# A retention layer feeding a two-matrix MLP: first loads spread over three queues, state sums ahead of outputs, and transposes and loads grouped by two pairs

## The chip, the cores and the metric

The kernel runs on one core of one Trainium2 chip. The metric is the device time of one execution in microseconds (us). Eight executions of the kernel before the change took 209.01 to 209.62 us, with a median of 209.3 us. One further execution was recorded by the profiler; it took 209.35 us, and its span, from the first to the last instruction, is 207.5 us.

## The reference

For each of 4 batch entries and 8 heads, a state of 64 x 64 is carried along 768 time steps. At each step it decays, takes up the outer product of k and v, and is read by q. The result, 3072 tokens of 512 features, goes through two matrices with x cos x between them.

```python
batch, n_heads, seq, head_dim = (4, 8, 768, 64)
n_tokens, d_model, d_ff = (3072, 512, 2048)

gamma = 1.0 - 2.0 ** (-5.0 - np.arange(H, dtype=np.float32))
scale = 1.0 / np.sqrt(D)
for t in range(S):
    state = gamma[None, :, None, None] * state + np.einsum('bhd,bhe->bhde', k[:, :, t], v[:, :, t])
    y[:, :, t] = scale * np.einsum('bhd,bhde->bhe', q[:, :, t], state)

h = x @ w_in          # x is y, heads side by side
g = h * np.cos(h)
out = g @ w_out
```

## The kernel before

The 768 steps are cut into six chunks of 128. Two batch entries are worked on together, so that there are 12 *pairs* p: two batch entries (b is 0 or 1) of one chunk, all eight heads. Pairs 0 to 5 are the six chunks of the first two entries, 6 to 11 those of the others. Decay is put into q and k beforehand, as powers of gamma, so that inside a chunk the recurrence becomes masked matrix products.

A pair goes through these steps, each a helper in the code:

- `load` brings q, k and v from memory, 256 KB for one b of one tensor. `load_k` brings both b of k in one transfer. A pair lands in one of five buffer slots, by the table `SLOT`.
- `conv_q`, `conv_k` and `conv_v` scale and turn to bf16: q and k into `qk`, v into `vs` (three buffers each, by p % 3). From pair 3 on q and v are converted on GpSimd (POOL) and k on ScalarE (ACT).
- `stage_t` transposes q and k of one b on TensorE (PE) and copies the result out on VectorE (DVE) into `qkt`. `stage_t_dma` does the same with two transposing transfers on SyncE's queue (SP). Pairs 0 to 3 use the first, 4 to 11 the second.
- `stage_a` is A, the products of k and q inside the chunk (two PSUM banks per b); `stage_m` multiplies them by the triangular mask on VectorE into `am`. `attend` is both, for both b.
- `half_y` is Y: the older state (`stb`) times q plus v times `am`, for one b; ScalarE copies the result into `xt`. `stage_s` is S: it adds the chunk's k-v products to the state in `st_ps` and copies it to `stb`. `stage_y` is Y of both b, then S.

Two pairs make a group g of 512 tokens for the MLP. `unit_f` computes one block f of 128 of the 2,048 hidden features for all 512 tokens; `act` takes the cosine on ScalarE and multiplies on VectorE into `gt`. `pair_f(p, r)` does four blocks for one pair alone (256 tokens), two blocks to a bank, and `first_f` for the first four blocks. `unit_o` multiplies `gt` with a quarter of `w_out` for 128 tokens; after the fourth quarter ScalarE copies the bank to `ob` and SP stores it. `warm` issues matrix products whose result nobody uses.

The program writes out the order of work on every engine by hand; each engine takes its instructions in that order, and an instruction whose input or buffer is not ready holds up those behind it. There are seven PSUM banks beside `st_ps`. `Banks.take` picks the bank that the written plan (`Clock`) expects to come free first; the numbers of `Clock` choose banks, not the order. The semaphores are put in from the data that instructions touch.

Around the change: in the beginning SP loads q and k of pair 0 and POOL the rest. S of pair 0 stands between the two Y of pair 0 on TensorE, and its copies behind the first `xt` copy on ScalarE. In the middle, q of pairs 4 and 5 and one v are loaded on SP, the rest on POOL; from pair 6 on POOL issues six loads for one pair, two conversions of q and two of v, then the next pair's six loads. The functions `ahead`, `fetch` and `later` place them at steps s of the main loop over groups.

Of the kernel before, what the change touches and what calls it, by code (L numbers as in the profile page):

```python
# [10 lines left out]
FP32 = mybir.dt.float32  # L11
# [36 lines left out]
def kernel(  # L48
# [32 lines left out]
    def sb(shape, dt, name):  # L81
        return const.tile(shape, dt, name=name)
# [14 lines left out]
    w_out_sb = sb([128, KOUT, DM], BF16, "w_out_sb")  # L97


    qf = [[sb([128, H, D], FP32, f"qf{i}_{b}") for b in range(2)] for i in range(PRE)]  # L100
    kf2 = [sb([128, 2, H, D], FP32, f"kf{i}") for i in range(PRE)]
    kf = [[t[:, b] for b in range(2)] for t in kf2]
    vf = [[sb([128, H, D], FP32, f"vf{i}_{b}") for b in range(2)] for i in range(PRE)]
    ob = [sb([128, DM], FP32, f"ob{i}") for i in range(4)]
    NB = 3
    qk = [sb([128, 2, 2, H, D], BF16, f"qk{i}") for i in range(NB)]
# [11 lines left out]
    gq = sb([128, NC, H], FP32, "gq")  # L118
    gk = sb([128, NC, H], FP32, "gk")
    rel = sb([128, 128], FP32, "rel")  # L120


    SRC = {"q": (qf, q), "k": (kf, k), "v": (vf, v)}
# [3 lines left out]
    def load(eng, p, names):  # L127
        bp, c = divmod(p, NC)
        for n in names:
            t, src = SRC[n[0]]  # L130
            b = int(n[1])
            eng.dma_start(  # L132
                out=t[SLOT[p]][b],
                in_=src[2 * bp + b, :, ds(c * C, C)].rearrange("h t d -> t h d"))

    def load_k(p):
        bp, c = divmod(p, NC)
        nc.gpsimd.dma_start(
            out=kf2[SLOT[p]].rearrange("p b h d -> p (b h) d"),
            in_=k[2 * bp : 2 * bp + 2, :, ds(c * C, C)].rearrange("b h t d -> t (b h) d"))  # L140

    def load_w_in(r):
        nc.gpsimd.dma_start(
# [14 lines left out]
    def w_in_t(i, f):  # L158
# [1 line left out]
        return w.rearrange("p (m j) -> p j m", j=4)[:, f % 4, :]  # L160


    load(nc.sync, 0, ("q0", "k0", "q1"))
    nc.gpsimd.iota(pos, pattern=[[C, NC]], base=1, channel_multiplier=1,
                   allow_small_or_imprecise_dtypes=True)
    nc.gpsimd.iota(rel, pattern=[[1, 128]], base=0, channel_multiplier=-1,
                   allow_small_or_imprecise_dtypes=True)
    load(nc.gpsimd, 0, ("k1",))
    load(nc.gpsimd, 1, ("q0", "q1"))
    load_k(1)  # L170
    load(nc.gpsimd, 0, ("v0", "v1"))
    nc.vector.memset(zero, 0.0)
    nc.vector.memset(lnsc, math.log(scale))
# [76 lines left out]
    def stage_a(p, b):  # L250
        n = p % NB
        bk = [banks.take(), banks.take()]
        ap = [t.rearrange("p (a t) -> p a t", a=HP) for t in bk]
        for a in range(HP):
            for j in range(2):
                po = 64 * j
                nc.tensor.matmul(ap[j][:, a, :], lhsT=kt(n, b, a)[po : po + 64, :],  # L257
                                 rhs=qt(n, b, a)[po : po + 64, :],
                                 tile_position=(po, 0))
        clk.run("pe", 0.3)  # L260
        return b, bk, ap, clk.pe

    def stage_m(p, item, parts=(0, 1)):
        b, bk, ap, done = item
        for j in parts:
            nc.vector.tensor_tensor(  # L266
                out=am[p % 2][b][j], in0=ap[j],
                in1=mask.unsqueeze(1).to_broadcast([128, HP, 128]), op=ALU.mult)
            banks.give(bk[j], clk.run("dve", 0.64, done + 0.1))

    def half_y(p, b):
        c = p % NC
        n = p % NB
        bank = banks.take()
        yp = bank.rearrange("p (a t) -> p a t", a=HP)
        for a in range(HP):
            if c > 0:
                for j in range(2):
                    nc.tensor.matmul(  # L279
                        yp[ts(j, 64), a, :], lhsT=stb[p % 2][:, b, a, ts(j, 64)],  # L280
                        rhs=qt(n, b, a), start=True, stop=False,
                        skip_group_check=True)
            for j in range(2):
                nc.tensor.matmul(  # L284
                    yp[ts(j, 64), a, :], lhsT=vs[n][:, b, 2 * a + j, :],
                    rhs=am[p % 2][b][j][:, a, :], start=(c == 0), stop=True,
                    skip_group_check=True)
        nc.scalar.copy(out=xt[(p // 2) % 2][:, :, ts(2 * (p % 2) + b, C)], in_=yp)  # L288
        clk.run("pe", 0.5)
        banks.give(bank, clk.run("act", 0.6, clk.pe + 0.1))  # L290

    def stage_s(p, copy_st):
        c = p % NC
        n = p % NB
        if c == NC - 1:
            return
        for b in range(2):
            for a in range(HP):
                for j in range(2):
                    h = 2 * a + j  # L300
                    nc.tensor.matmul(  # L301
                        st_ps[ts(j, 64), b, a, :], lhsT=qk[n][:, b, 1, h, :],
                        rhs=vs[n][:, b, h, :], start=(c == 0 and b == 0 and a == 0),
                        stop=True, skip_group_check=True)
        clk.run("pe", 0.25)
        if copy_st is not None:
            state_out(p, copy_st)
# [103 lines left out]
    def warm(n):  # L411
        for _ in range(n):
            nc.tensor.matmul(spare, lhsT=zero[:, :128], rhs=zero, start=True, stop=True,
                             skip_group_check=True)
        clk.run("pe", 0.3 * n)
# [47 lines left out]
    warm(1)  # L463
    clk.run("pe", 0.0, 11.8)
    stage_m(1, stage_a(1, 0))
    half_y(0, 0)
    clk.run("pe", 0.0, 12.4)
    stage_m(1, stage_a(1, 1))
    stage_s(0, nc.scalar.copy)
    half_y(0, 1)  # L470
    warm(3)
    half_y(1, 0)
    banks.give(spare, clk.pe)
    half_y(1, 1)
    stage_s(1, nc.scalar.copy)
# [6 lines left out]
    for u in range(12):  # L482
        unit_o(0, u % 4, u // 4)
        if u == 7:
            stage_t(2, 0)
            stage_t(2, 1)
            conv_v(2, nc.vector, (0,))
        elif u == 9:
            stage_m(2, stage_a(2, 0))
            conv_v(2, nc.vector, (1,))  # L490
        elif u == 11:
            stage_m(2, stage_a(2, 1))
    conv_k(3, True)
    conv_q(3, nc.gpsimd)
    load(nc.sync, 4, ("q0", "q1"))
    load(nc.gpsimd, 4, ("k0", "k1", "v0", "v1"))
    conv_v(3, nc.gpsimd)
    load(nc.sync, 5, ("q0", "q1", "v0"))
    load(nc.gpsimd, 5, ("k0", "k1", "v1"))
    for j in range(4):  # L500
        unit_o(0, j, 3)
        if j == 1:
            stage_y(2, nc.scalar.copy)
    pair_f(2, 0)
    stage_t(3, 0)
    stage_t(3, 1)
    pair_f(2, 1)
    attend(3)
    conv_q(4, nc.gpsimd)
    conv_v(4, nc.gpsimd)  # L510
    conv_k(4, True)
    stage_t_dma(4)
    load(nc.gpsimd, 6, ("q0", "k0", "q1", "k1", "v0", "v1"))
    pair_f(2, 2)
    pair_f(2, 3, (0,))
    stage_y(3, nc.scalar.copy)
    pair_f(2, 3, (1,))
    conv_q(5, nc.gpsimd)
    conv_v(5, nc.gpsimd)
    load(nc.gpsimd, 7, ("q0", "k0", "q1", "k1", "v0", "v1"))  # L520
    pair_f(3, 0)
    conv_k(5, True)
    stage_t_dma(5)
    pair_f(3, 1)
    pair_f(3, 2)
    conv_q(6, nc.gpsimd)
    conv_k(6, True)
    conv_v(6, nc.gpsimd)
    pair_f(3, 3)

    def ahead(p):
        if p < NP:
            conv_q(p, nc.gpsimd)
            conv_k(p, True)
            conv_v(p, nc.gpsimd)

    def fetch(p):
        load(nc.gpsimd, p, ("q0", "k0", "q1", "k1", "v0", "v1"))

    def later(p):  # L540
        stage_y(p)
        n = 8 if p == 4 else p + 3 if p > 5 else NP
        if n < NP:
            fetch(n)

    late = []

    def put_off(when, step):
        late.append((when, step))
# [13 lines left out]

    o_units(1, 0, 2)
    attend(4)
    stage_t_dma(6)
    o_units(1, 2, 6)
    later(4)
    attend(5)
    o_units(1, 6, 10)  # L570
    later(5)

    for g in range(2, NG + 1):
        for s in range(16):
            hf, r = divmod(s, 8)
            p = 2 * (g + 1) + hf
            if g == 2 and s % 2 == 0 and s < 12:
                unit_o(1, *divmod(10 + s // 2, 4))
            if g < NG:
                unit_f(g, s)  # L580
            if g > 2:
                if g < NG or s < 12:
                    unit_o(g - 1, *divmod(s, 4))
                elif s == 12:
                    last_o(g - 1, 3)
            while late and late[0][0] <= 16 * g + s:
                late.pop(0)[1]()
            if p < NP:
                if r == 0:
                    ahead(p + 1)  # L590
                elif r == 1:
                    if p + 1 < NP:
                        stage_t_dma(p + 1)
                elif r == 2 and p in (6, 7, 8):
                    todo = [stage_a(p, b) for b in range(2)]
                    stage_m(p, todo[0])
                    put_off(16 * g + s + 1, lambda todo=todo, p=p: stage_m(p, todo[1]))
                elif r == 6 and p in (6, 7, 11):
                    later(p)
                elif (g, s) == (3, 4):  # L600
                    fetch(11)
                if (g, s) in joined:
                    join(joined[g, s], 16 * g + s)


# [28 lines left out]
```

## Time and profile before

| what | value |
|---|---|
| median of 8 runs | 209.3 us (209.01 to 209.62) |
| profiled execution | 209.35 us, its span 207.5 us |
| TensorE busy | 201.2 us, 97% of the span |
| VectorE, ScalarE, GpSimd busy | 112.7, 114.3, 102.5 us |
| chain that ended last | 92% TensorE, 3% DMA, 2% VectorE |
| software queue (POOL's transfers) | 20.98 MB, 38.1% of 16 engines' span |
| hardware queue (SP's transfers, the transposes among them) | 12.49 MB, 26.2% |
| clock granted to TensorE | 1.00 |

Busy time of an engine is the union of its instructions; for TensorE their ends are modelled. The chain of waits goes back from the last instruction, at each step to what released it or to the instruction before it on its engine. A timeline row gives the start and length of some instructions in a row, what they write and read, and in brackets how long the engine was idle before and what ended that. The landing time of a transfer is from its issue to its last byte; the answers give the least, the median and the largest of those asked for.

### The profile page before, as it was taken

To read this page: it belongs to the slowest core of one execution; us is meant where nothing else is said; L and a number is where in the kernel's file an instruction comes from. 1 tells how busy PE (TensorE), PEld (TensorE's weight loads), DVE (VectorE), ACT (ScalarE), POOL (GpSimd) and SP (SyncE) were. 2 spreads that over 40 slices of the span, in tenths; PEclk is the share of its full clock that TensorE was granted. 3 is DMA by queue.
4 is the path that set the end of the run, shared out by engine and by line. 5 is a ranking of instruction groups with operands and counts; after the bars stand their busy time and mean duration, and the time that the engine had idled before them with its cause. 6 is when DMAs were issued, how large, how long until landed. Compare 5 with 4: busy or idle time off the path is not lost.

```text
span 207.5 us, 4176 instructions
## 1 busy us (share of the span) xinstructions
PE 201.2 (97%) x1646; PEld 113.3 (55%) x1646; DVE 112.7 (54%) x188; ACT 114.3 (55%) x193; POOL 102.5 (49%) x118
## 2 busy tenths in 40 slices
PE   7889999999999999999999999999999999999993
PEld 3357554558997555546544466444465444444452
DVE  4691984544957454869874466853467244443000
ACT  6677872257996336577653754653554653553120
POOL 8999238399999999999998030000000000000000
PEclk9999999999999999999999999999999999999999
DMA  6999999999999999979997411161101100110212
GB/s 153 336 241 202 215 241 287 335 279 328 252 218 280 293 216 298 215 244 181 210 272 243 121 37 48 57 101 51 51 3 51 51 20 34 51 52 21 80 75 79
DMA packets 36644, 33.83 MB, mean 163 GB/s; under 512 B 26768, under 2 KB 29072, under 8 KB 36624
## 3 DMA queue, kind: packets, MB, share of 16 engines
q0 software_dynamic: 7808, 20.98, 38.1%
q1 hardware_dynamic: 28672, 12.49, 26.2%
q8 instruction: 13, 0.21, 0.4%
q10 hardware_dynamic: 144, 0.10, 0.1%
q14 instruction: 7, 0.06, 0.1%
HBM read 27.26 MB, written 6.29 MB: 162 GB/s over the span
## 4 chain that ended last, share of the span: by engine, by line
PE 92%; DMA 3%; DVE 2%; issue 1%; SPq 0%; ACT 0%; DVEq 0%
PE bank L379 39%; PE bank L338 32%; PE bank L349 7%; PE bank L257 3%; DMA qf<-in_q_dram 3%; PE bank L279 3%; PE bank L284 3%; PE bank L396 2%; PE st_ps L301 1%; DVE am L266 1%; PE bank L360 1%; PE bank L230 1%; PE bank L367 1%; DVE qkt L214 1%; SPq L132 0%
## 5 line engine op out<-in xcount | busy, mean ns | idle before, releaser
L331 DVE TENSOR_TENSOR gt<-bank,cosb 128x512 bf16<-128x512 f32 x96 | 64.8, 688 | 62.3 <-ACT cosb L327 62.0
L327 ACT ACTIVATE cosb<-bank,halfpi 128x512 bf16<-128x512 f32 x96 | 65.1, 688 | 49.9 <-PE bank L338 45.5
L379 PE MATMUL bank<-w_out_sb,gt 128*128 128x512 bf16 x368 | 89.6, 379 | 0.0
L338 PE MATMUL bank<-xt,w_in 128*128 128x512 bf16 x304 | 75.3, 380 | 0.0
L379 PEld LDWEIGHTS <-gt 128*128 128x128 bf16 x368 | 35.4, 98 | 41.3
L338 PEld LDWEIGHTS <-w_in 128*128 128x128 bf16 x304 | 33.7, 114 | 30.9
L266 DVE TENSOR_TENSOR am<-bank,mask 128x512 bf16<-128x512 f32 x48 | 30.4, 682 | 4.2 <-PE bank L257 4.2
L202 POOL TENSOR_TENSOR vs<-vf,gk 128x512 bf16<-128x512 f32 x21 | 21.4, 1041 | 7.3 <-PE st_ps L301 7.2
L386 ACT COPY ob<-bank 128x512 f32<-128x512 f32 x23 | 13.4, 586 | 18.1 <-PE bank L379 18.0
L132 POOL DMA_DIRECT2D vf<-in_v_dram x23 | 20.2, 884 | 4.5 <-DMA w_out_sb<-in_moe_w_out_dram 4.5
L195 POOL TENSOR_TENSOR qk<-qf,gq 128x512 bf16<-128x512 f32 x18 | 18.8, 1068 | 2.9 <-DMA qf<-in_q_dram 2.2
L132 POOL DMA_DIRECT2D kf<-in_k_dram x21 | 18.9, 900 | 1.8 <-DMA w_out_sb<-in_moe_w_out_dram 1.6
L208 ACT CAST qk<-kf 128x512 bf16<-128x512 f32 x24 | 13.9, 615 | 9.2 <-DMA kf<-in_k_dram 9.2
L288 ACT CAST xt<-bank 128x512 bf16<-128x512 f32 x24 | 13.0, 588 | 7.7 <-PE bank L284 7.6
L132 POOL DMA_DIRECT2D qf<-in_q_dram x18 | 16.2, 901 | 1.3 <-DMA w_in<-in_moe_w_in_dram 1.3
L349 PE MATMUL bank<-xt,w_in 128*128 128x256 bf16 x128 | 14.7, 273 | 0.0
L349 PEld LDWEIGHTS <-w_in 128*128 128x128 bf16 x128 | 13.8, 114 | 0.4
L284 PE MATMUL bank<-am,vs 128*64 128x128 bf16 x192 | 11.7, 220 | 0.0
L279 PEld LDWEIGHTS <-stb 128*64 128x64 bf16 x160 | 8.8, 109 | 4.3 <-issue 3.1
L279 PE MATMUL bank<-qkt,stb 128*64 128x128 bf16 x160 | 10.7, 222 | 0.1
L284 PEld LDWEIGHTS <-vs 128*64 128x64 bf16 x192 | 10.0, 110 | 0.5 <-issue 0.4
L313 DVE CAST stb<-st_ps 64x512 bf16<-64x512 f32 x12 | 8.2, 684 | 2.7 <-PE st_ps L301 2.6
(46 smaller groups left out, 87.0 us busy)
## 6 DMA issues: line engine op xcount, KB each, us to landing
vf<-in_v_dram POOLq DMA_DIRECT2D x23, 256.0 KB, 6.2
out_dram<-ob SPq DMA_DIRECT2D x23, 256.0 KB, 2.0
kf<-in_k_dram POOLq DMA_DIRECT2D x21, 256.0 KB, 6.5
qf<-in_q_dram POOLq DMA_DIRECT2D x18, 256.0 KB, 5.9
w_out_sb<-in_moe_w_out_dram POOLq DMA_DIRECT2D x4, 512.0 KB, 12.4
qf<-in_q_dram SPq DMA_DIRECT2D x6, 256.0 KB, 7.7
w_in<-in_moe_w_in_dram POOLq DMA_DIRECT2D x3, 512.0 KB, 8.7
kf<-in_k_dram POOLq DMA_DIRECT2D x1, 512.0 KB, 5.9
```

The source lines that it names most:

```text
L132: eng.dma_start(out=t[SLOT[p]][b], in_=src[2 * bp + b, :, ds(c * C, C)].rearrange("h t d -> t h d"))
L195: eng.tensor_tensor(out=qk[p % NB][:, b, 0], in0=qf[SLOT[p]][b], in1=bc(gq, p % NC), op=ALU.mult)
L202: eng.tensor_tensor(out=vs[p % NB][:, b], in0=vf[SLOT[p]][b], in1=bc(gk, p % NC), op=ALU.mult)
L208: nc.scalar.copy(out=qk[p % NB][:, b, 1], in_=kf[SLOT[p]][b])
L266: nc.vector.tensor_tensor(out=am[p % 2][b][j], in0=ap[j], in1=mask.unsqueeze(1).to_broadcast([128, HP, 128]), op=ALU.mult)
L279: nc.tensor.matmul(yp[ts(j, 64), a, :], lhsT=stb[p % 2][:, b, a, ts(j, 64)], rhs=qt(n, b, a), start=True, stop=False, skip_group_check=True)
L284: nc.tensor.matmul(yp[ts(j, 64), a, :], lhsT=vs[n][:, b, 2 * a + j, :], rhs=am[p % 2][b][j][:, a, :], start=(c == 0), stop=True, skip_grou ...
L327: nc.scalar.activation(out=cb, in_=bank, func=AF.Sin, bias=halfpi)
L331: nc.vector.tensor_tensor(out=out, in0=bank, in1=cb, op=ALU.mult)
L338: nc.tensor.matmul(bank, lhsT=w_in_t(i, f), rhs=xt[g % 2][:, i, :], start=(i == 0), stop=(i == KIN - 1))
L349: nc.tensor.matmul(bank[:, ts(e, 256)], lhsT=w_in_t(i, f + e), rhs=xt[g % 2][:, i, ts(hf, 256)], start=(i == 0 and e == 0), stop=(i == KIN ...
L379: nc.tensor.matmul(bank, lhsT=gt[g % 2][:, f, ts(j, 128)], rhs=w_out_sb[:, f, :], start=(f == 0), stop=(f == KOUT - 1))
```

## The change

- At the start, k of pair 0 (b = 0) is issued on ScalarE's hardware queue, ahead of ScalarE's first table load. SP issues q of pair 0 and then q of pair 1 (b = 0 each). The second q of pair 0 goes to POOL, behind the second k.
- S of pair 0 moves ahead of both Y of pair 0, and both Y behind both A of pair 1. Of the three `warm` products one stays ahead of pair 1's first Y and two go between its two Y.
- q, k and v of all slots become tiles that hold both b, and from pair 4 on each is loaded by one transfer of 512 KB on POOL (`load_both`). SP no longer loads in the middle.
- Pair 3 is transposed by transfers. A new function `turn` takes one or two pairs: q conversions, transposing transfers of all of them on SP, v conversions, then on POOL a copy of two elements (`gate`) out of the last pair's first transposed half, and behind that the loads for the next two pairs in the order k, q, k, q, v, v.
- The k conversions on ScalarE get places of their own: that of pair 3 at u = 9, that of pair 4 behind `pair_f(2, 0)`, that of pair 5 behind `attend(3)`, later ones by a table `k_at`. The tables `t_at`, `a_at` and `y_at` take the place of `ahead`, `fetch` and `later`.

```diff
-    load(nc.sync, 0, ("q0", "k0", "q1"))
+    load(nc.scalar, 0, ("k0",))
+    load(nc.sync, 0, ("q0",))
+    load(nc.sync, 1, ("q0",))
...
-    load(nc.gpsimd, 0, ("k1",))
-    load(nc.gpsimd, 1, ("q0", "q1"))
-    load_k(1)
+    load(nc.gpsimd, 0, ("k1", "q1"))
+    load(nc.gpsimd, 1, ("q1",))
+    load_both(("k", 1))
...
     stage_m(1, stage_a(1, 0))
+    stage_s(0, nc.scalar.copy)
+    clk.run("pe", 0.0, 13.0)
+    stage_m(1, stage_a(1, 1))
     half_y(0, 0)
-    clk.run("pe", 0.0, 12.4)
-    stage_m(1, stage_a(1, 1))
-    stage_s(0, nc.scalar.copy)
     half_y(0, 1)
-    warm(3)
+    warm(1)
     half_y(1, 0)
+    warm(2)
     banks.give(spare, clk.pe)
     half_y(1, 1)
...
             conv_v(2, nc.vector, (1,))
+            conv_k(3, True)
...
-    conv_k(3, True)
-    conv_q(3, nc.gpsimd)
-    load(nc.sync, 4, ("q0", "q1"))
-    load(nc.gpsimd, 4, ("k0", "k1", "v0", "v1"))
-    conv_v(3, nc.gpsimd)
-    load(nc.sync, 5, ("q0", "q1", "v0"))
-    load(nc.gpsimd, 5, ("k0", "k1", "v1"))
+    def turn(ps, loads=()):
+        for p in ps:
+            conv_q(p, nc.gpsimd)
+        for p in sorted(ps):
+            stage_t_dma(p)
+        for p in sorted(ps):
+            conv_v(p, nc.gpsimd)
+        if loads:
+            nc.gpsimd.tensor_copy(out=gate, in_=qkt[max(ps) % NB][:, 0, 1, HP - 1, 126:])
+            load_both(*[(n, p) for n, p in (
+                ("k", 0), ("q", 0), ("k", 1), ("q", 1), ("v", 0), ("v", 1)) for p in [loads[p]]])
+
+    turn((3,), (4, 5))
...
     pair_f(2, 0)
-    stage_t(3, 0)
-    stage_t(3, 1)
+    conv_k(4, True)
     pair_f(2, 1)
     attend(3)
-    conv_q(4, nc.gpsimd)
-    conv_v(4, nc.gpsimd)
-    conv_k(4, True)
-    stage_t_dma(4)
-    load(nc.gpsimd, 6, ("q0", "k0", "q1", "k1", "v0", "v1"))
+    conv_k(5, True)
+    turn((5, 4), (6, 7))
...
+    k_at = {(2, 6): 8, (2, 9): 9, (3, 2): 10, (3, 12): 11}
+    t_at = {(2, 9): ((8, 9), (10, 11)), (3, 3): ((10,),), (3, 13): ((11,),)}
+    a_at = {(2, 2): 6, (2, 10): 7, (3, 2): 8}
+    y_at = {(2, 6): 6, (2, 14): 7, (4, 14): 11}
```

More of the change, by code (lines that the diff above doesn't have):

```diff
@@ L97 @@
     w_out_sb = sb([128, KOUT, DM], BF16, "w_out_sb")
[L100 to L103, printed above, removed]
+    both = {n: [sb([128, 2, H, D], FP32, f"{n}f{i}") for i in range(PRE)] for n in "qkv"}
+    qf, kf, vf = [[[t[:, b] for b in range(2)] for t in both[n]] for n in "qkv"]
     ob = [sb([128, DM], FP32, f"ob{i}") for i in range(4)]
@@ L120 @@
     rel = sb([128, 128], FP32, "rel")
+    gate = sb([128, 2], BF16, "gate")
     SRC = {"q": (qf, q), "k": (kf, k), "v": (vf, v)}
@@ L134, in load, with load_both @@
                 in_=src[2 * bp + b, :, ds(c * C, C)].rearrange("h t d -> t h d"))
[L136 to L140, printed above, removed]
+    def load_both(*names):
+        for n, p in names:
+            bp, c = divmod(p, NC)
+            nc.gpsimd.dma_start(
+                out=both[n][SLOT[p]].rearrange("p b h d -> p (b h) d"),
+                in_=SRC[n][1][2 * bp : 2 * bp + 2, :, ds(c * C, C)].rearrange(
+                    "b h t d -> t (b h) d"))
     def load_w_in(r):
@@ L517 @@
     pair_f(2, 3, (1,))
-    conv_q(5, nc.gpsimd)
-    conv_v(5, nc.gpsimd)
-    load(nc.gpsimd, 7, ("q0", "k0", "q1", "k1", "v0", "v1"))
     pair_f(3, 0)
-    conv_k(5, True)
-    stage_t_dma(5)
     pair_f(3, 1)
     pair_f(3, 2)
-    conv_q(6, nc.gpsimd)
-    conv_k(6, True)
-    conv_v(6, nc.gpsimd)
     pair_f(3, 3)
[L531 to L544, printed above, removed]
     late = []
@@ L565 @@
     attend(4)
-    stage_t_dma(6)
     o_units(1, 2, 6)
-    later(4)
+    conv_k(6, True)
+    stage_y(4)
     attend(5)
+    conv_k(7, True)
+    turn((6, 7), (8, 9))
     o_units(1, 6, 10)
-    later(5)
+    stage_y(5)
+    k_at = {(2, 6): 8, (2, 9): 9, (3, 2): 10, (3, 12): 11}
+    t_at = {(2, 9): ((8, 9), (10, 11)), (3, 3): ((10,),), (3, 13): ((11,),)}
+    a_at = {(2, 2): 6, (2, 10): 7, (3, 2): 8}
+    y_at = {(2, 6): 6, (2, 14): 7, (4, 14): 11}
     for g in range(2, NG + 1):
         for s in range(16):
-            hf, r = divmod(s, 8)
-            p = 2 * (g + 1) + hf
             if g == 2 and s % 2 == 0 and s < 12:
@@ L585 @@
                     last_o(g - 1, 3)
-            while late and late[0][0] <= 16 * g + s:
+            now = 16 * g + s
+            while late and late[0][0] <= now:
                 late.pop(0)[1]()
[L588 to L603, printed above, removed]
+            at = (g, s)
+            if at in k_at:
+                conv_k(k_at[at], True)
+            if at in t_at:
+                turn(*t_at[at])
+            if at in a_at:
+                p = a_at[at]
+                todo = [stage_a(p, b) for b in range(2)]
+                stage_m(p, todo[0])
+                put_off(now + 1, lambda todo=todo, p=p: stage_m(p, todo[1]))
+            if at in y_at:
+                stage_y(y_at[at])
+            if at in joined:
+                join(joined[at], now)
 _INS = ['q', 'k', 'v', 'moe_w_in', 'moe_w_out']
```

## The prediction

> **What bounds the kernel now.** I read the page's busy times first, then the chain of waits in order of time, then the timelines of ScalarE, VectorE, GpSimd and SyncE wherever that chain leaves TensorE, and last the landing times of single transfers.
>
> The page's head, part 1 and the engine line of part 4:
>
> ```profile
> span 207.5 us, 4176 instructions
> ...
> PE 201.2 (97%) x1646; PEld 113.3 (55%) x1646; DVE 112.7 (54%) x188; ACT 114.3 (55%) x193; POOL 102.5 (49%) x118
> ...
> PE 92%; DMA 3%; DVE 2%; issue 1%; SPq 0%; ACT 0%; DVEq 0%
> ```
>
> TensorE is 92% of the chain. Time can only be won by work taken off TensorE, or ahead of about 16 us where others carry the chain; it is lost wherever TensorE is made to wait. The chain (start, length, what):
>
> ```profile
> 1.88 5.76 DMA qf<-in_q_dram
> ...
> 8.28 1.28 DVE am L266 x2
> ...
> 14.70 0.59 ACT stb L313
> ...
> 16.66 1.87 PE bank L360 x16
> ...
> 47.57 1.75 PE bank L349 x16
> 49.32 0.89 PE bank L230 x16
> ...
> 55.87 0.19 PE bank L284 x2
> ...
> 56.65 7.98 PE bank L349 x72
> ```
>
> First the late second q, then VectorE with hardly a gap to 13 us, then the state copy; first_f begins at 16.66. At 49.32 stand pair 3's transposes, 0.89. The 0.19 at 55.87, where others take 0.06, is Y of pair 3 waiting for its last masked product. The nine half units from 56.65 give pair_f(3,0) a start of 56.65 + 0.87 = 57.52: my anchor.
>
> ScalarE, then VectorE, around that place:
>
> ```profile
> 49.41 0.69 ACT L327 ACTIVATE cosb<-bank,halfpi 128x512 bf16<-128x512 f32 x1 [0.20 <-PE bank L349]
> 51.18 1.50 ACT L327 ACTIVATE cosb<-bank,halfpi 128x512 bf16<-128x512 f32 x2 [1.08 <-PE bank L349]
> 52.58 1.13 ACT L208 CAST qk<-kf 128x512 bf16<-128x512 f32 x2
> ...
> 53.32 2.47 DVE L266 TENSOR_TENSOR am<-bank,mask 128x512 bf16<-128x512 f32 x4
> ```
>
> Pair 4's k is cast without a wait, after the cosines that pair 3's masks queue behind; the masks end at 55.79. Now GpSimd:
>
> ```profile
> 41.92 1.38 POOL L195 TENSOR_TENSOR qk<-qf,gq 128x512 bf16<-128x512 f32 x1 [0.61 <-DVE am L266]
> 43.24 1.80 POOL L132 DMA_DIRECT2D kf<-in_k_dram  x2
> ...
> 74.10 0.92 POOL L132 DMA_DIRECT2D qf<-in_q_dram  x1
> ```
>
> Today pair 4's k loads are issued at 43.24, ahead of pair 3's v.
>
> **What the Trainium skill says.** "PSUM — Partial Sum Buffer", section "Engine vs sequencer instructions": the queues of ScalarE, VectorE and GpSimd are strict FIFO. The trace agrees: ScalarE stood 4.9 us at pair 3's k cast with nothing passing it. "SBUF — State Buffer", section "SBUF: two separate sides": a VectorE operation with two SBUF inputs and a GpSimd operation exclude each other. It agrees: pair 3's second q conversion took 1.38 instead of 1.04 while VectorE's v conversion (41.71, 0.68) ran. "Advanced Engine Details and Errata", section "X-Bar Transpose (TRN2)": transposing transfers are as fast as plain ones. Only alone: such a transfer lands in 2.8 us at 71.19, but in 6.8 at 53.27 among loads, and all DMA falls to 27 GB/s from 56 to 57 us. "DMA: Bandwidth & Descriptors", section "Queues, rings and completion order": an engine serves its rings in turn, packet by packet, so a store takes turns from loads. The loads beside the two stores at 73.93 agree (7.2 us below).
>
> **The front, part by part.** k of pair 0 goes to ScalarE's queue ahead of the table load (1.28). One issue costs 0.46 to 0.57, so the exponentials at 2.46 may slip 0.1; conv_q at 3.91 covers that, and without cover it costs 0.1. Two hardware rings now share the engines: k lands before 5.20, the first q after 3.82. Both are hidden, because VectorE's next hard date is the second q at 7.64. That q is now POOL's second issue, at 2.43; today's transfer in that slot took 5.37 and landed at 7.80. Same bytes, same slot: I take no shift, with ends -0.3 and +0.3. The q of pair 1 on SP feeds ScalarE, which then waits for k at 10.09 anyway: nothing.
>
> S ahead of Y: today S is done at 14.07, the copies at 15.27, and Y of pair 1 runs 15.33 to 16.39. Then: A ends 12.94, S (0.39) 13.3, the two copies (1.18) 14.5, meanwhile the other A and Y of pair 0 (0.33 + 2 x 0.34) and one warm-up (0.27). Half of Y of pair 1 takes 0.53, to 15.1; two warm-ups 15.6; the other half waits for the last mask (13.07 + 2.47 = 15.54) and ends at 16.14; S 0.27: first_f at 16.41. **Gain 0.25.** w_in's parts land at 15.25 and 16.51, in time. xt waits behind the stb copies, yet its last copy, at 16.75, comes before first_f's second half.
>
> **Pair 3's transposes** leave TensorE: -0.89; two copies of VectorE go too (1.28, from 50.74). Its k cast moves up on ScalarE to the load's landing (40.94 at the latest), where ScalarE idles: nothing. Together with the front that is 1.14, of which the mask chain keeps most even if all data are in time. Cosine of pair_f(2,0) 49.16; pair 4's k cast now stands right behind it, 49.75 to 50.8 (two, 1.03 apart in all); two cosines, 50.8 and 51.4; the second product at 52.1; four masks at 0.6, the last ends at 55.24 instead of 55.79. **Net gain there 0.55**, and a late k4 takes it away one for one after 49.75.
>
> **When k4 and k5 land.** GpSimd's second q conversion ends at 43.3 as now, conv_v (2.05) at 45.35. The gate copy (two elements; nearest row the 0.15 iota; nothing to 0.2) waits for pair 3's first transposed half, and behind it on GpSimd stand all six loads and the conversions of pairs 5 and 4. That half is issued at 41.4; alone 2.8 gives 44.2, among loads 6.8 gives 48.2. Only v3's tail (landing 43.4) is in its way, so I take it as in by 45.4. First load issue at **45.5**, where pair 4's k has 43.24 and its q, on SP, earlier dates. On SP the two new transposes (1.23 to 2.7 of issue each) stand ahead of unit 0's four stores; SP's loads that stand there today let the first store out at 44.71, so about the same. The stores then take turns with the loads. What that does is seen in the run of six loads at 74.10, beside two stores: its first two loads, and its last two, land after
>
> ```profile
> DMA to landing us min/median/max: 4.5/5.4/6.3
> ...
> DMA to landing us min/median/max: 5.9/5.9/6.0
> ```
>
> The second is issued at 75.02, the sixth at 78.52, so 512 KB are in 7.2 and 1.5 MB 10.3 after the first issue. Read the same way, the run at 64.80 (no store) takes 5.2 (65.72 + 4.3) and 8.4 (69.21 + 4.0), that at 83.40 (a store and a transpose) 7.4 and 10.9.
> The merged loads carry the same bytes in half the issues (1.15 against 2 x 0.88). That saves GpSimd 1.9 a pair, but landing, not issue, sets these runs, so I count nothing. The middle of the runs at 64.80 and 74.10: k4 at 45.5 + 6.2 = 51.7, k5, third in the list, at 45.5 + 9.35 = 54.85.
>
> From k4: -0.55 + (51.7 - 49.75) = **+1.4**. From k5: its cast stands ahead of the cosines of pair_f(2,2). Two casts 1.03, three cosines at 0.62, two xt copies 0.56 + 0.58 and some 0.1 of hand-over make 4.1 before pair_f(3,0) may read xt: 58.95 against 57.52, **+1.4** too. TensorE is in order and full afterwards, so it stays.
>
> **Later groups.** q5 56.4, four q conversions to 60.4, transposes of 4 and 5 from 59.5 at 1.4 each: pair 4's land by 63.7, needed at 66.4: hidden. Next gate 65.2, loads of 6 and 7 issued to 72.2, pair 6's transposes issued 73.3 and 74.7 among loads that land until 78.3. By the row at 80.50 (1.0 after the last load, the next 2.1 later) they land at 79.3 and 81.4, needed at 81.28 + 1.4: hidden by 1.3, but with the worst row, 8.7, late by 0.5. Casts of 8 to 11 and their transposes have one to several us and seven banks as cover. The casts no longer ahead of pair_f(3) free ScalarE where it has room: nothing.
>
> Sum: profiled 209.35 (span 207.5 and 1.85 around it) + 1.4 = 210.75; the median is 209.3, so 210.7.
>
> **Rivals.** *Loads in time* (the other side): with no store in the way k4 needs its issue, 1.15, then 2.7 to its landing (the load at 92.69: 3.6 less 0.92 of issue) and 0.6 for its further bytes: 49.95; k5 follows two more of 1.53 (pair 1's k landed that long after the load before it): 53.0. It decides at k4 before 50.3 and k5 before 53.4; fully so, -0.4 to -0.55: 208.8. For it: pair 4's and 5's loads on SP are gone, and two stores may be through first. Against: all three runs above. *Cancelled*: k4 within 0.4 of 50.3 or k5 of 53.4: 209.3. *The transposes late*: pair 3's first half lands as at 53.27, at 48.2, so the loads start at 48.3 and everything moves 2.8; or pair 6's stop A by a us or two. 212 to 213.5. Against: only v3's tail is in flight.
>
> **How the numbers follow.** Half for the forecast (209.9 to 212), 0.16 for late transposes, 0.15 cancelled, 0.19 in time. A measurement of this kernel can tell about 0.2%, 0.4 us. Low end: all in time, and 0.1 from the front, 208.7. High end: the slower run, 10.9, gives k5 56.4 and +3.0; with transposes half a us late 212.8. Beyond lie about 0.07 and 0.11. The forecast's own range is 209.9 to 212.
>
> **What would show it.** first_f at about 16.4; no L230 row between the first two units of pair_f(2); ScalarE idle before the casts of k4 and k5 with a DMA named, about 2 and 0.5 to 1 us; masks ending near 57; pair_f(3,0) near 59; then no gap of TensorE. Wrong if no load waits are seen there, if the second q lands over 0.5 away from 7.7, or if TensorE stops at pair 6's A.

## The result, and the profile after

The changed kernel takes **212.62 us** (median of 11 runs, 212.07 to 214.35), the kernel before 209.32 in the runs beside it. The ratio is 1.0174, with a 95% interval of 1.0159 to 1.0190. By the medians 3.3 us are lost, where 1.4 was forecast, with 209.9 to 212 as its range. Four of the kernels below scatter by several us from run to run, the ratios leave out runs that took over 1.5% more than their kernel's fastest, and the profiles of three of the four (pair 3's transposes by DMA, the late casts, every cast late) are of such longer runs, so that they show a mechanism and not a median.

The profiled execution took 212.39 us. Its page, head, part 1 and the engine line of part 4:

```profile
span 210.6 us, 4105 instructions
...
PE 201.0 (95%) x1630; PEld 112.9 (54%) x1630; DVE 112.3 (53%) x186; ACT 114.6 (54%) x193; POOL 93.2 (44%) x103
...
PE 52%; DMA 22%; POOL 14%; issue 5%; DVE 3%; ACT 3%; POOLq 0%; DVEq 0%; ACTq 0%
```

TensorE is as busy as before (201.0 against 201.2 us), in a span 3.1 us longer. Its share of the chain of waits fell from 92% to 52%: until 101 us the chain now runs mostly through GpSimd and DMA. The chain in order of time (start, length, what):

```profile
44.62 5.82 DMA kf<-in_k_dram
...
50.99 0.61 ACT qk L211
51.60 0.60 ACT cosb L330
...
53.43 1.89 DVE am L269 x3
...
55.65 0.61 ACT qk L211
56.26 1.36 ACT cosb L330 x3
...
59.02 3.60 PE bank L352 x32
62.63 2.73 DMA qkt<-qk
...
66.10 1.19 POOL kf L138
...
69.57 5.38 DMA qf<-in_q_dram
74.95 1.00 POOL qk L198
...
80.77 4.06 DMA qkt<-qk
...
87.85 7.46 DMA kf<-in_k_dram
...
100.06 1.21 DVE am L269 x2
```

Read it as two rounds of one cycle: six loads, the conversion of q, the transposes, the gate, and the next six loads. TensorE appears between 59 and 62.6 us, but other rows show that the transposes did not wait for it: q of pair 5 landed at 56.60, GpSimd converted from 56.74 on, and SP issued the four transposes from 59.80, each right behind the one before; the one at 62.63 is the third. Where TensorE itself stood still, its timeline shows (in brackets the idle time before the row, and what ended it):

```profile
52.97 1.91 PE L352 MATMUL bank<-xt,w_in 128*128 128x256 bf16 x16 [0.72 <-DVE gt L334]
55.95 0.22 PE L287 MATMUL bank<-am,vs 128*64 128x128 bf16 x1 [0.38 <-DVE am L269]
59.02 7.15 PE L352 MATMUL bank<-xt,w_in 128*128 128x256 bf16 x64 [1.27 <-ACT xt L291]
84.11 0.40 PE L260 MATMUL bank<-qkt 64*128 64x128 bf16 x8 [0.96 <-DMA qkt<-qk]
101.31 0.22 PE L287 MATMUL bank<-am,vs 128*64 128x128 bf16 x1 [0.38 <-DVE am L269]
```

The first three are the masks, cosines and xt copies behind pair 4's and 5's k casts. The row at 59.02 is pair_f(3,0), at 57.52 before: +1.50. The fourth is A of pair 6, whose second transposed half landed at 84.06. The fifth is Y of pair 7. What each costs is read from the rows behind it, first in the kernel before, then in the changed one:

```profile
64.47 1.89 PE L379 MATMUL bank<-w_out_sb,gt 128*128 128x512 bf16 x8
...
81.77 1.05 PE L338 MATMUL bank<-xt,w_in 128*128 128x512 bf16 x4
...
98.59 1.92 PE L338 MATMUL bank<-xt,w_in 128*128 128x512 bf16 x8
```

```profile
66.00 1.89 PE L382 MATMUL bank<-w_out_sb,gt 128*128 128x512 bf16 x8
...
84.44 1.05 PE L341 MATMUL bank<-xt,w_in 128*128 128x512 bf16 x4
...
102.04 1.92 PE L341 MATMUL bank<-xt,w_in 128*128 128x512 bf16 x8
```

TensorE is 1.53 late behind the first three, 2.67 behind A of pair 6 (+1.14) and 3.45 behind Y of pair 7 (+0.78: 0.55 at the row shown, the rest in rows just ahead of it and behind it). It stays 3.46 late to its last matrix products. The spans differ by 3.1 only, because the changed kernel ends 0.3 sooner after its last store is issued.

ScalarE around the first three:

```profile
50.46 1.14 ACT L211 CAST qk<-kf 128x512 bf16<-128x512 f32 x2 [0.73 <-DMA kf<-in_k_dram]
51.51 1.26 ACT L330 ACTIVATE cosb<-bank,halfpi 128x512 bf16<-128x512 f32 x2
55.12 1.14 ACT L211 CAST qk<-kf 128x512 bf16<-128x512 f32 x2 [2.36 <-DMA kf<-in_k_dram]
56.17 1.84 ACT L330 ACTIVATE cosb<-bank,halfpi 128x512 bf16<-128x512 f32 x3
57.89 1.08 ACT L291 CAST xt<-bank 128x512 bf16<-128x512 f32 x2
```

Both casts wait for their loads, with cosines and xt copies queued behind them. GpSimd at the next turn:

```profile
60.74 4.04 POOL L205 TENSOR_TENSOR vs<-vf,gk 128x512 bf16<-128x512 f32 x4
65.48 0.19 POOL L506 COPY gate<-qkt 128x2 bf16<-128x2 bf16 x1 [0.69 <-DMA qkt<-qk]
66.10 1.19 POOL L138 DMA_DIRECT2D kf<-in_k_dram  x1 [0.44 <-issue]
...
73.91 2.04 POOL L198 TENSOR_TENSOR qk<-qf,gq 128x512 bf16<-128x512 f32 x2 [0.91 <-DMA qf<-in_q_dram]
```

The gate and what follows it put 1.3 us between the last v conversion (64.78) and the first load. Pair 6's q conversion waits for its q, and only then can its transposes be issued (74.98 and 76.40). They run among the remaining loads. From issue to landing, the four transfers of pairs 4 and 5 (first fence, from 59.8 us, when only the last 0.9 us of a load is in their way) and the two of pair 6 (second):

```profile
DMA to landing us min/median/max: 2.7/2.7/2.8
```

```profile
DMA to landing us min/median/max: 6.7/7.2/7.7
```

### The profile page after: what moved, and what is told of

The parts are those of the page before. It is cut to its first block, busy times and chain, and to the rows that moved or that the text cites. A ratio compares the mean times of both kernels' runs of the same rounds, so it can differ in the third digit from the quotient of the medians.

```text
span 210.6 us, 4105 instructions
## 1 busy us (share of the span) xinstructions
PE 201.0 (95%) x1630; PEld 112.9 (54%) x1630; DVE 112.3 (53%) x186; ACT 114.6 (54%) x193; POOL 93.2 (44%) x103
## 4 chain that ended last, share of the span: by engine, by line
PE 52%; DMA 22%; POOL 14%; issue 5%; DVE 3%; ACT 3%; POOLq 0%; DVEq 0%; ACTq 0%
PE bank L382 25%; PE bank L341 20%; DMA w_out_sb<-in_moe_w_out_dram 7%; DMA kf<-in_k_dram 6%; DMA qf<-in_q_dram 6%; DMA qkt<-qk 3%; POOL vs L205 2%; POOL kf L138 2%; DVE am L269 2%; PE bank L352 2%; PE bank L399 2%; POOL vf L131 2%; POOL qk L198 1%; POOL kf L131 1%; POOL qf L131 1%
## 5 line engine op out<-in xcount | busy, mean ns | idle before, releaser
L334 DVE TENSOR_TENSOR gt<-bank,cosb 128x512 bf16<-128x512 f32 x96 | 64.9, 689 | 66.4 <-ACT cosb L330 66.1
L198 POOL TENSOR_TENSOR qk<-qf,gq 128x512 bf16<-128x512 f32 x18 | 18.4, 1041 | 12.9 <-PE st_ps L304 5.2
L138 POOL DMA_DIRECT2D kf<-in_k_dram x9 | 10.5, 1167 | 1.2 <-issue 0.8
L260 PE MATMUL bank<-qkt 64*128 64x128 bf16 x192 | 8.1, 218 | 2.2 <-DVE qkt L217 1.1
L416 PE MATMUL bank<-gt 128*128 128x512 bf16 x22 | 8.1, 478 | 1.2 <-DVE gt L175 1.2
```

The lines of the kernel that those rows point to most:

```text
L138: nc.gpsimd.dma_start(out=both[n][SLOT[p]].rearrange("p b h d -> p (b h) d"), in_=SRC[n][1][2 * bp : 2 * bp + 2, :, ds(c * C, C)].rearrang ...
L198: eng.tensor_tensor(out=qk[p % NB][:, b, 0], in0=qf[SLOT[p]][b], in1=bc(gq, p % NC), op=ALU.mult)
L334: nc.vector.tensor_tensor(out=out, in0=bank, in1=cb, op=ALU.mult)
```

## The experiments

The theory after the traces: each two-pair turn is a chain of its own (loads, conversion of q, transposes, gate), and TensorE loses where an engine in order meets data of a turn that is late; taking one such wait away leaves the turn's dates, so another takes its place. The first rival: the waits are separate and add up.

### The front alone

```diff
 the kernel before, with
-    load(nc.sync, 0, ("q0", "k0", "q1"))
+    load(nc.scalar, 0, ("k0",)); load(nc.sync, 0, ("q0",)); load(nc.sync, 1, ("q0",))
-    load(nc.gpsimd, 0, ("k1",)); load(nc.gpsimd, 1, ("q0", "q1"))
+    load(nc.gpsimd, 0, ("k1", "q1")); load(nc.gpsimd, 1, ("q1",))
 and S of pair 0, A of pair 1 ahead of Y of pair 0, warm-ups 1 + 2
```

> The kernel before with the front edits alone (order of the first loads, S of pair 0 ahead of its Y, the warm-ups split). Theory 1 (the front gains what the prediction said, and TensorE keeps it to the end): first_f 0.25 to 0.5 us earlier, 208.8 to 209.1 us against 209.3 of before. Rival (the data behind it, the loads of pairs 2 and 3 or the transposes of pair 3, take it back): no measurable difference, 209.3 plus or minus 0.1, with a new wait of TensorE somewhere between 15 and 55 us.

Measured: 209.00 us (208.87 to 209.33), ratio 0.9982 (0.9969 to 0.9996). Its chain:

```profile
2.43 4.80 DMA qf<-in_q_dram
...
12.19 0.40 PE bank L259 x8
12.58 0.42 PE st_ps L303 x16
...
16.27 1.76 PE bank L362 x15
```

first_f begins 0.39 us earlier than before (16.66), and no wait of TensorE follows: the end comes 0.39 earlier. One profile each is thin evidence for so little, since the row of first_f starts between 16.20 and 16.69 in the ten profiles with the new front and at 16.43 and 16.59 in the two with the old; the gain rests on the 21 runs, whose interval leaves 0.1 to 0.6 us. The second q lands at 7.23 instead of 7.64, so the two edits of the front both move the first A and S; how the 0.39 divides between them was not tried.

### The turns alone

```diff
 the changed kernel, with the front of the kernel before
```

> The changed kernel with the front of the kernel before, so the two-pair turns of DMA alone. Theory 1 (the whole loss is in the turns; the turns begin with pair 3's conversions on GpSimd, which move with TensorE's schedule): 212.8 to 213.1 us, the front's gain above the changed kernel. Rival (the turns run at their own pace whatever TensorE does, so a later TensorE waits less for them): 212.6, no difference from the changed kernel.

Measured: 212.10 us, ratio 1.0135 (1.0112 to 1.0158): not slower than the changed kernel, rather 0.4% faster. Theory 1's number fell and the rival's is nearer. TensorE starts first_f later here, yet pair 6's second half lands at 83.99 us, as in the changed kernel (84.06), and TensorE waits 0.60 for it instead of 0.96. The turns keep their own dates here; the front's gain is waited away. Y of pair 7 doesn't wait here; k of pair 9 landed 0.9 earlier (94.43 against 95.31), for which nothing in the edit gives a reason.

### The casts of k later

```diff
-    conv_k(4, True)            # behind pair_f(2, 0)
     pair_f(2, 1)
     attend(3)
-    conv_k(5, True)
-    turn((5, 4), (6, 7))
+    conv_k(4, True)
     pair_f(2, 2)
     pair_f(2, 3, (0,))
     stage_y(3, nc.scalar.copy)
     pair_f(2, 3, (1,))
+    conv_k(5, True)
+    turn((5, 4), (6, 7))
```

> The changed kernel with ScalarE's casts of pair 4's k behind the masks of pair 3 and of pair 5's k behind the last half unit of pair_f(2), so that no cosine stands behind a cast whose load is late. Theory 1 (the turns chain themselves: loads of 6 and 7 and pair 6's transposes keep their dates of 66.1 and 84.06 us): pair_f(3,0) starts at 57.0 to 57.6 instead of 59.02, but pair 6's second A still waits for its transposes at 84 us, so TensorE's wait there grows from 1.1 to about 2.5, and the time falls by 0.3 at most: 212.3 to 212.7 us. Rival (the three waits of TensorE add): the 1.5 to 2 us come back in full, 210.6 to 211.1 us.

Measured: 212.89 us, ratio 1.0166 (1.0144 to 1.0187). The three waits before 60 us are gone and pair_f(3,0) starts at 56.4, 2.6 us earlier, and nothing of it reaches the end. TensorE's later waits:

```profile
73.87 1.89 PE L382 MATMUL bank<-w_out_sb,gt 128*128 128x512 bf16 x8 [0.79 <-ACT xt L291]
...
79.84 1.89 PE L341 MATMUL bank<-xt,w_in 128*128 128x512 bf16 x8 [2.10 <-ACT xt L291]
...
84.20 0.40 PE L260 MATMUL bank<-qkt 64*128 64x128 bf16 x8 [0.74 <-DMA qkt<-qk]
85.13 0.40 PE L260 MATMUL bank<-qkt 64*128 64x128 bf16 x8 [0.54 <-DMA qkt<-qk]
```

4.2 us of idle time in their place. The second turn's loads start at 66.50, not earlier than in the changed kernel (66.10). The casts of pair 6's and pair 7's k now stand waiting for their loads (landed 72.17 and 77.13) with xt copies behind them, and pair 6's transposes land at 84.16 and 85.09. The theory of the chain holds in what it says of the dates, that of added waits falls. The theory's details were off: pair_f(3,0) came earlier than it had, only 1.3 of the idle time stands at pair 6's A, not 2.5, and the time is just above its range.

### Without the stores of group 0

```diff
-            nc.sync.dma_start(out=dst, in_=o)
+            if g > 0:
+                nc.sync.dma_start(out=dst, in_=o)
```

> The changed kernel without the four stores of group 0 (rows 0 to 511 of the output are not written), which run beside the loads of pairs 4 and 5. Theory 1 (the stores take turns with these loads): k of pair 4 lands 0.5 to 1 us earlier than 50.44, k of pair 5 1 to 1.5 us earlier than 55.10, pair_f(3,0) starts near 57.8, the gate of the next turn and with it pair 6's transposes come about 1 us earlier, and the time is 211.0 to 211.7 us. Rival (six merged loads land at their own pace, stores or not): landings within 0.3 us of the changed kernel's and 212.4 to 212.7 us.

(The rows not written are 0 to 255 of each of the first two batch entries, not 0 to 511.) Measured: 210.94 us, ratio 1.0071 (1.0049 to 1.0093): 1.7 us back. From issue to landing, the six loads of pairs 4 and 5 in the changed kernel, and then without the stores:

```profile
DMA to landing us min/median/max: 5.8/8.3/10.4
```

```profile
DMA to landing us min/median/max: 5.1/7.2/8.1
```

The first is k of pair 4. The loads began at 45.07 here instead of 44.62, so by the clock k of pair 4 gained only 0.24 and k of pair 5 0.72, and pair_f(3,0) starts at 58.30; these landings gained less than expected. The last v gained 1.8, the next turn's loads began 0.8 earlier (65.32), and pair 6's A waits 0.70. Y of pair 7 doesn't wait. So with the four stores of 256 KB single loads of this turn take 0.2 (q of pair 4) to 2.3 us (v of pair 5) longer, and half of the loss goes with the stores.

### The first turn alone

```diff
 the changed kernel up to attend(3) and conv_k(5), then as in the kernel before:
-    turn((5, 4), (6, 7))
+    conv_q(4, nc.gpsimd); conv_v(4, nc.gpsimd)
+    stage_t_dma(4)
+    load(nc.gpsimd, 6, ("q0", "k0", "q1", "k1", "v0", "v1"))
     ...                        # pairs 5 to 11 one by one
```

> The changed kernel up to pair 5 (front, pair 3's transposes by DMA, gate, six merged loads of pairs 4 and 5, casts of their k where the change puts them), and from pair 6 on the loads and conversions pair by pair as in the kernel before. Theory 1 (the later turns cost by themselves: pair 6's transposes land late because its loads begin only when the transposes of 4 and 5 are in): the wait at pair_f(3,0) stays (start 58.9 to 59.3), TensorE doesn't wait at pair 6's A nor at pair 7's Y, and the time is 210.6 to 211.0 us. Rival (the waits of 82.9 and 100.7 are only what the first delay pushes on, and pairs loaded one by one are as late): 212.2 to 212.8 us.

Measured: 210.93 us, ratio 1.0074 (1.0052 to 1.0095), as theory 1 had it: pair_f(3,0) at 59.16, and no wait of TensorE over 0.2 us after it. This divides the loss, in the order front, first turn, later turns: -0.4, +1.9 (209.0 to 210.9) and +1.7 (210.9 to 212.6). In another order the shares differ: put on top of the turns, the front costs 0.5 (212.1 to 212.6) instead of gaining 0.4.

### No gate

```diff
-            nc.gpsimd.tensor_copy(out=gate, in_=qkt[max(ps) % NB][:, 0, 1, HP - 1, 126:])
```

> The changed kernel without the two-element copy on GpSimd that holds each turn's loads back until the last pair's transposes are in. Theory 1 (the turn is bound by its own chain, loads 10 us, conversions of q 4 us, transposes 5.5 us, and the gate is only the last 0.6 to 1.3 us of it): loads of 6 and 7 start near 64.9 instead of 66.10, pair 6's transposes land at most 1 us earlier, 211.8 to 212.4 us. Rival A (the gate is what makes the turn long): more than 1 us back, under 211.6 us. Rival B (loads run into the transposes in flight and slow both): 212.6 us or more.

Measured: 211.58 us, ratio 1.0113 (1.0093 to 1.0133): 1.0 us back, just inside rival A's number and outside theory 1's, though the interval reaches into both. The gate costs about a third of the loss. The second turn's loads start at 64.73 instead of 66.10, and pair 6's transposes land at 80.39 and 82.75, both 1.3 earlier. A of pair 6 is then one row:

```profile
82.46 0.74 PE L260 MATMUL bank<-qkt 64*128 64x128 bf16 x16
```

So 1.3 us at the start of the turn is what A of pair 6 lacked; Y of pair 7 doesn't wait either. Loads that started beside the last two transposes did them no harm (2.7 us each). One turn later rival B shows in part: the six loads that start at 81.99 beside two transposes take 7.4 to 9.8 us to land, against 5.4 to 8.8 with the gate. The wait at pair_f(3,0) is still there (58.73).

### Three tries for a faster kernel, and the merged loads

First, pair 3's transposes by DMA, loads one pair at a time as before, and no gate:

```diff
 the front alone, with
     load(nc.sync, 4, ("q0", "q1"))
+    stage_t_dma(3)
-    stage_t(3, 0)
-    stage_t(3, 1)
 and conv_k(3) two units earlier, as in the change
```

> The front edits and pair 3's transposes by DMA, with the loads of pairs 4 and 5 as in the kernel before (pair by pair, no gate). Theory 1 (pair 3's transposes are issued near 41 to 43 us among loads, and land in 7 to 9 us, at about 50, when its A is due; the loads behind lose little): TensorE gains the 0.89 us of the transposes beside the front, 207.9 to 208.4 us. Rival (transposes among loads slow all transfers, so pair 3's A waits or pair 4's k comes late for its cast, which stands behind A there): 208.8 to 210.5 us, with a wait at pair 3's A near 50 us.

Measured: 216.06 to 253.59 us in six runs, median 239.68. Both theories fall. Pair 3's own transposes land in time (48.6 and 50.5), but those of pairs 4 to 6 then meet loads, and loads and transposes slow each other. From issue to landing of the transposes of pairs 5 and 6, and TensorE at A of pairs 4 and 5:

```profile
DMA to landing us min/median/max: 14.2/16.2/18.4
```

```profile
70.19 0.61 PE L259 MATMUL bank<-qkt 64*128 64x128 bf16 x8 [4.56 <-DMA qkt<-qk]
...
82.51 0.60 PE L259 MATMUL bank<-qkt 64*128 64x128 bf16 x8 [4.59 <-DMA qkt<-qk]
```

Loads issued from 65 to 75 us take 13 to 14.5 us, where in the changed kernel they take 5 to 9. Why this order is slowed so much, and the kernel before, which also transposes among loads, isn't in its profiled run, stays open.

Second, the first turn alone with its k casts late:

```diff
 the first turn alone, with
-    conv_k(4, True)            # behind pair_f(2, 0)
-    conv_k(5, True)            # behind attend(3)
+    conv_k(4, True)            # behind attend(3)
+    conv_k(5, True)            # behind pair_f(3, 0)
```

> The kernel of the first turn alone (pair by pair from pair 6 on), with the casts of pair 4's k behind pair 3's masks and of pair 5's k behind pair_f(3,0), as in the kernel before. Theory 1 (the waits at 51.97, 55.36 and 57.48 us come from these casts standing ahead of cosines while their loads are late; with the turns gone nothing takes the place of that wait): pair_f(3,0) starts at 56.9 to 57.4, and the time is 208.3 to 208.9 us, under both kernels. Rival (as with the casts moved in the changed kernel, the delay comes back at the next thing that waits for DMA, near 70 to 85 us): 210 us or more.

Measured: 213.23 us (210.36 to 215.30), ratio 1.0097 (1.0065 to 1.0129). pair_f(3,0) starts at 57.13, then the rival's case: ScalarE, and TensorE behind it:

```profile
67.87 0.62 ACT L211 CAST qk<-kf 128x512 bf16<-128x512 f32 x1 [4.51 <-DMA kf<-in_k_dram]
70.61 0.62 ACT L211 CAST qk<-kf 128x512 bf16<-128x512 f32 x1 [2.12 <-DMA kf<-in_k_dram]
```

```profile
72.59 1.71 PE L382 MATMUL bank<-w_out_sb,gt 128*128 128x512 bf16 x4 [4.20 <-DVE gt L334]
```

The loads of pair 6 began at 62.83 (55.08 with the front alone), because GpSimd's v conversion of pair 4 stood ahead of them and its v was late; pair 6's k cast then held two cosines.

Third, from the kernel just shown, the casts of pairs 4 and 6 moved too, so that every cast of pairs 4 to 6 stands behind what it could hold up:

```diff
-    conv_k(4, True)            # behind attend(3)
-    stage_t_dma(4)
+    conv_k(4, True)            # behind the last half unit of pair_f(2)
+    stage_t_dma(4)
     conv_k(5, True)            # behind pair_f(3, 0), as it was
-    conv_k(6, True)            # behind pair_f(3, 2)
+    conv_k(6, True)            # behind attend(4)
```

> As the run with the late casts of k of pairs 4 and 5, with two more casts moved: pair 4's k behind the last half unit of pair_f(2), pair 6's k behind the masks of pair 4 (in that run ScalarE stood from 63.3 to 70.6 us at the cast of pair 6's k with two cosines of pair_f(3,3) queued behind it). Theory 1 (each stall is a cast in ScalarE's queue ahead of a cosine or an xt copy; with none left in such a place the 0.89 us of pair 3's transposes stays off TensorE): pair_f(3,0) starts at 56.3 to 56.6 us, no wait of TensorE over 0.5 us after it, 208.2 to 208.7 us. Rival (the later loads move the wait to transposes of pair 5 or 6 instead): a wait at an A between 66 and 83 us, 209.5 to 212 us.

Measured: 211.28 us (208.71 to 214.92), ratio 1.0044 (1.0017 to 1.0071). In the profiled run no cast holds TensorE, and the wait has gone to A of pair 5 (0.97 and 0.41) and of pair 6:

```profile
84.89 0.40 PE L260 MATMUL bank<-qkt 64*128 64x128 bf16 x8 [2.92 <-DMA qkt<-qk]
```

The rival again. The last, merging without turns:

```diff
 the front alone, with
-    load(nc.gpsimd, p, ("q0", "k0", "q1", "k1", "v0", "v1"))
+    load_both(("q", p), ("k", p), ("v", p))      # pairs 6 to 11
```

> The front edits alone, with the loads of pairs 6 to 11 merged two by two as in the change (q, k and v of both batches in one transfer each), in the order and at the places of the kernel before. Theory 1 (merging changes the issue time on GpSimd, 3 x 1.15 instead of 6 x 0.88 us a pair, and not the landing): 208.8 to 209.2 us, no difference from the front alone. Rival (a merged load lands later than its first half did, so casts and conversions wait): 209.6 us or more.

Measured: 210.23 us (208.86 to 217.06), ratio 1.0005 (0.9966 to 1.0043): seven of 14 runs took 208.9 to 209.5, the others 211.0 and more. In the profiled one TensorE waits 1.85 at A of pair 8, and the transposes issued from 79 to 96 us take 10.2 to 13.6 us to land and loads 9.3 to 14.5, as in the first try. Inconclusive: merging costs nothing in half the runs and scatters in the others. The kernel before scatters beside these last two as well, with 8 of 34 runs at 210.8 to 216.1, so that the scatter is not of the edits alone. Of all kernels run, the front alone is the only one faster than both.

## Why the prediction was right or wrong

**The front: right in sign, two terms mis-sized.** The second q was given no shift, with ends of 0.3; it landed 0.45 earlier (4.75 us from issue instead of 5.37). first_f was put at 16.41 and came at 16.27 in the run of the front alone. Alone it is worth 0.38, not 0.25.

**Pair 3's transposes: right.** The L230 rows between the first units of pair_f(2) are gone, and the casts of k hold the cosines that the masks queue behind.

**k4 wrong, k5 right.** Loads began at 44.62 (forecast 45.5), since the v conversion ended earlier. k4 took 5.82 (6.2) and landed at 50.44, not 51.7, so the masks end at 55.90 and not near 57: of its +1.4 only 0.1 came, against 55.79 before. k5 took 10.48 from the first issue (9.35) and landed at 55.10, forecast 54.85: a start too late and a run too short nearly cancelled. From there to pair_f(3,0) it was 3.92 (forecast 4.1), which gives 59.02 for 58.95. The sum took the two terms of 1.4 as one, so k5 alone carries it. That the stores take turns with these loads, as "DMA: Bandwidth & Descriptors", section "Queues, rings and completion order", of the Trainium skill has it, fits the run without them: 5.13 and 9.31 instead of 5.82 and 10.48.

**Later groups: the step that failed.** The forecast had no loss here, and two of its sentences fail. "Hidden by 1.3": the first load was put at 65.2 and came at 66.10 (of this, 0.44 between gate and load had no term). The six loads were given 13.1 us from the first issue to the last landing, with no working shown; in the three turns they took 16.1, 14.7 and 14.5. q's conversion was put right behind the last issue at 72.2; it had to wait for q6 until 73.91. The loads were to land by 78.3 and did at 80.81, and the transposes landed 0.85 and 3.25 after that (1.0 and 3.1 in the forecast): 81.66 and 84.06, not 79.3 and 81.4. So the landing of the last load is the mis-sized term, and the row that placed the transposes behind it was sound: in the runs without the front, with the casts late, without the stores and without the gate the first half also lands 0.85 to 0.98 after the last load of that turn. Against the need, 82.7 for A's first half in the forecast and some 0.3 later for its second, that cost 1.1. "Casts of 8 to 11 ... have one to several us and seven banks as cover": pair 9's k, cast at 95.33 on landing, held cosines and masks of pair 7, and Y of pair 7 stood for 0.55 (0.8 with the rows around it). Here the place of the cast is at fault more than the ring, since A of pair 9 begins only at 124; a later place with the turns kept was not tried. Each is small; together they are 1.9 us of TensorE's time, put at nothing, of which 0.3 come back at the end. The profiled run is 1.64 above its forecast of 210.75.

**Signs of being wrong.** Two of the three that it named came: TensorE stopped at pair 6's A, and the second q landed at 7.19, just over 0.5 from 7.7.

**Rivals.** What came is the likeliest case and the second half of "transposes late" at once, at its 212 to 213.5. They were weighed as if one excluded the other, though the late loads of one turn also delay the next. Loads in time and cancelled are refuted by the rows at 55.12 and 59.02.

## What to carry to other kernels

Where loads, conversions and transposes wait for each other in a ring, work out the period of the ring and its dates in every round, not only in the first; a wait that is removed ahead of it comes back at its next date. Here the first loads of the turns start at 44.62, 66.10, 85.52 and 104.73, so two pairs take 21.5 to 19.2 us, where the kernel before issues a pair's loads every 9.3 us (64.80, 74.10, 83.40): one turn for two pairs is no faster than two pairs one by one. TensorE began A of pairs 4, 6 and 8 at 66.4, 81.3 and 104.8 in the kernel before, 14.9 and 23.5 us apart, so that only the first of these two steps asks for more than the ring gives. A cast in an in-order queue costs nothing while its data are early, and all that stands behind it when they aren't: look at what is queued behind every instruction that waits for a load. A gain ahead of the ring (the front's 0.38) is kept only while the ring has slack.

## What was not expected of the hardware

Transposing transfers and loads slow each other without a bound that this case shows: 2.7 us alone, 6.7 to 7.7 beside the loads of one turn, 14.2 to 18.4 in the first of the three tries, where loads took 13 to 14.5 instead of 5 to 9. "Advanced Engine Details and Errata", section "X-Bar Transpose (TRN2)", of the Trainium skill has them as fast as plain transfers. That agrees with the first number only: the quickest plain load of 256 KB in the kernel before, issued at 0.74, landed in 3.1 us.

TensorE's granted clock fell after the longest waits. In the run with every cast late, in the 5 us after the wait of 2.92 (columns: stretch, sum, busy time and count of PE, PEld, DVE, ACT, POOL, granted clock, DMA share, GB/s):

```profile
86.00:91.00 5.00, 5.00 (x17) 1.94 (x15) 2.45 (x4) 1.74 (x3) 5.00 (x6) 0.66 1.13 254
```

Matrix products of 512 columns then start 0.43 us apart instead of 0.22. The run with the late casts shows 0.66 too, from 72 to 77 us behind its wait of 4.20, and the one with pair 3's transposes by DMA 0.50 from 82 to 87 us around the end of its wait of 4.59. After the waits of 1.27 in the changed kernel, 1.85 in the run with merged loads and 2.10 in the run with the casts of k later the clock stayed at 1.00. So in these runs a wait of some 3 us and more cost more than its own length; where between 2.10 and 2.92 that begins, and whether the length alone decides, no run shows.
